# GELU of the w_in product: one ScalarE GELU from PSUM in place of four operations on two engines

## The chip, the core and the metric

The kernel runs on one core of one Trainium2 chip. The metric is the device time of one execution in microseconds (us). One core has several engines, each with its own instruction queue: TensorE (PE, matmuls), VectorE (DVE), ScalarE (ACT), GpSimd (POOL) and SyncE (SP, which starts most DMAs). VectorE and ScalarE take their queues in order. The Trainium skill says so ("TensorE: Matmul & The Clock Gate", section "Architectural detail: the array is 16× 32×32, not 1× 128×128": "ACT/DVE are strict FIFO").

## The reference

A transformer block on 2048 tokens of width 1024: an attention part (A), then a gated MLP (B). The change touches only the start of B, where `_gelu` is the tanh approximation:

```python
z  = gelu(layernorm(h) @ w_in, approximate=True)   # 2048 x 3584
z1 = z[..., :1792]
z2 = layernorm(z[..., 1792:])
g  = w_sp @ z2 + b_sp[:, None]                     # mixes tokens, w_sp is 2048 x 2048
out = h + (z1 * g) @ w_out
```

## The kernel before

The w_in stage works in four segments of 512 tokens. A segment has 30 blocks: 14 blocks "z1" (128 features x 512 tokens, written to their final place) and four token chunks of four blocks "z2" (128 tokens x 512, 512, 512 and 256 features). The four z2 blocks of a chunk go to one buffer, `Z2G`; then VectorE and GpSimd do the LayerNorm of the chunk (`z2_ln`), and the buffer is free again. Between two z2 chunks lie three or four z1 blocks. The units in `xu` make the next segment's input: `hn1` is its LayerNorm (VectorE), `hn2` its transposes (TensorE) and a copy (VectorE). There are 8 PSUM banks, taken in turn.

Each block is 8 matmuls into one bank. The GELU is then 0.5 x (1 + tanh(...)), with the factor 0.5 left for later:

```python
def z2_ln(tc, t4):                      # VectorE: 4 statistics, ..., normalise into Z2
    t = ln_stats(Z2G, 4, 4.0 * LN_EPS, [t4], csz=448)
    tz = P("dve", ... tensor_scalar(Z2[:, tc, :], Z2G[:], ...), waits=[t], sig=g_dve_pe)
    z2g_res.free = (g_dve_pe, tz[1])
# [cut]
blocks = z2blocks[0] + z1blocks[0:4] + z2blocks[1] + z1blocks[4:8] + z2blocks[2] + \
         z1blocks[8:11] + z2blocks[3] + z1blocks[11:14]
prev = None
for n in range(len(blocks) + 1):
    blk = blocks[n] if n < len(blocks) else None
    if prev is not None:                # second half of the GELU, block n-1
        # [cut]
        t3 = P("act", ... activation(TH[g], WG[g], Tanh, scale=GELU_C),
               waits=[prev["t2"], th_res[g].free], sig=g_act_dve)
        wg_res[g].free = t3
        t4 = P("dve", ... scalar_tensor_tensor(out, TH[g], 1.0, dst, add, mult),
               waits=[t3], sig=g_dve_pe)
        th_res[g].free = t4
        misc[prev["mb"]].free = t4      # the PSUM bank is free
        if prev["kind"] == "z2" and prev["fb"] == 3:
            z2_ln(prev["tc"], t4)
            if xu: xu.pop(0)()
    if blk is not None:                 # matmuls and first half, block n
        # [cut]
        w = [misc[mb].free] + (wready if n == 0 else [])
        if blk["kind"] == "z2" and blk["fb"] == 0:
            w.append(z2g_res.free)      # TensorE waits for the z2 buffer
        tp = proj8(blk["lhs"], blk["rhs"], dst, w, g_pe_act)
        # [cut]
        t1 = P("act", ... activation(X2T[g], dst, Square), waits=[tp, x2t_res[g].free], ...)
        t2 = P("dve", ... scalar_tensor_tensor(WG[g], X2T[g], GELU_K, dst, add, mult),
               waits=[t1, wg_res[g].free], ...)
        x2t_res[g].free = t2
        blk["t2"] = t2
    prev = blk
    if blk is not None and blk["kind"] == "z1" and blk["fc"] % 2 == 1 and xu:
        xu.pop(0)()
```

`P(engine, ...)` appends one instruction to the queue of that engine, with the semaphores it waits for. So the order in which the Python code calls `P` is the order of each queue.

The softmax here doesn't subtract the row's maximum and nothing guards it: scores larger than these inputs give would overflow.

## Time and profile before

| | before |
|---|---|
| median of the first 3 runs | 1267.02 us (1263.14 to 1269.56) |
| profiled run, span | 1264.5 us |
| attention and the first LayerNorm of B, 0 to 597.5 us | 597.5 us |
| w_in stage, 597.5 to 931.8 us | 334.3 us |
| loading and transposing of w_sp | 19.0 us |
| w_sp and w_out | 313.7 us |

First some lines of the profile page of before: busy time and share of the span by engine, the granted TensorE clock in 40 slices (in tenths), and the chain that ended last, by engine.

```profile
span 1264.5 us, 16478 instructions
...
PE 978.3 (77%) x6735; PEld 490.3 (39%) x6848; DVE 672.3 (53%) x1688; ACT 361.8 (29%) x502; POOL 35.1 (3%) x68
...
PEclk9979897998879986567978888889869999999999
...
PE 48%; DVE 31%; ACT 11%; issue 4%; DMA 4%; POOL 2%; SPq 0%; DVEq 0%; ACTq 0%; POOLq 0%
```

TensorE is at 77%, VectorE at 53% over the whole. The next view cuts the span into the four stretches of the table; the columns are length, busy time of each engine with the count of instructions, mean granted clock, DMA share and GB/s.

```profile
core 0: us, PE busy (x) PEld busy (x) DVE busy (x) ACT busy (x) POOL busy (x), PEclk, DMA share, GB/s
0.00:597.50 597.50, 434.24 (x4128) 234.82 (x4194) 316.24 (x1060) 234.72 (x262) 18.66 (x39) 0.84 0.15 51
597.50:931.80 334.30, 234.74 (x1035) 106.67 (x1054) 236.53 (x452) 127.09 (x240) 15.33 (x28) 0.85 0.03 8
931.80:950.80 19.00, 7.35 (x64) 6.72 (x66) 5.53 (x8) 0.00 (x0) 1.12 (x1) 0.50 0.94 340
950.80:1264.50 313.70, 301.97 (x1508) 142.05 (x1534) 113.95 (x168) 0.00 (x0) 0.00 (x0) 0.99 0.15 47
```

In the w_in stage TensorE and VectorE are equally busy, 70% and 71%, at a clock of 0.85. In the last stretch TensorE is busy 96% at 0.99.

One block, from the timeline (start, length, engine, and in brackets the idle time before and what ended it):

```profile
623.81 0.63 ACT L828 ACTIVATE th_116<-wg_114 128x512 bf16<-128x512 bf16 x1 [3.11 <-DVE wg_114 L862]
...
624.47 0.69 DVE L833 SCALAR_TENSOR_TENSOR z1T<-th_116,ps 128x512 bf16<-128x512 bf16 x1 [0.70 <-ACT th_116 L828]
625.08 0.68 DVE L862 SCALAR_TENSOR_TENSOR wg_115<-x2t_112,ps 128x512 bf16<-128x512 bf16 x1
625.68 0.68 DVE L765 COPY hnT_104<-ps 128x1024 bf16<-128x1024 bf16 x1
625.79 0.63 ACT L828 ACTIVATE th_117<-wg_115 128x512 bf16<-128x512 bf16 x1 [0.87 <-DVE wg_115 L862]
...
626.46 0.69 DVE L833 SCALAR_TENSOR_TENSOR z1T<-th_117,ps 128x512 bf16<-128x512 bf16 x1
```

`wg` is the first multiply-add (0.68 us), `th` the tanh on ScalarE (0.63), `z1T` the second multiply-add (0.69).

The chain of waits within the stage, by line (L328 is the LayerNorm statistics, L833 the second multiply-add, L862 the first, L828 the tanh), goes back and forth between VectorE and ScalarE:

```profile
by line: DVE stats L328 15.1%; DVE z2g L833 11.7%; DVE z1T L833 11.0%; ACT th_116 L828 11.0%; DVE wg_114 L862 10.4%; DVE wg_115 L862 10.1%; ACT th_117 L828 9.5%; POOL sm_58 L333 4.7%; DVE z_106 L791 3.6%; issue 3.5%; DVE mv L330 2.1%; PE ps
```

TensorE's largest waits in the same stage, and the place in the timeline that shows one of them:

```profile
PE ps L391 <- DVE z_106 L791: 65.7, 12, 6.4
PE ps L344 <- DVE hn_109 L751: 16.1, 3, 6.0
```

```profile
637.90 0.75 DVE L791 TENSOR_SCALAR z_106<-z2g,sm_58 128x1792 bf16<-128x1792 bf16 x1
...
638.79 1.44 PE L391 MATMUL ps<-w_in_hi,hnT_103 128*128 128x512 bf16 x3 [6.43 <-DVE z_106 L791]
```

The first matmul of a z2 chunk waits 6.43 us until the LayerNorm has read the buffer (`z_106`).

### The profile page before, as it was taken

The numbers are of one execution on the slowest core, as the hardware profiler recorded it, in microseconds if no ns is written. First come the engines' busy times: TensorE is split into PE (matmuls) and PEld (weight loads), VectorE is DVE, ScalarE is ACT, GpSimd is POOL, SyncE is SP. The second block draws the span as 40 slices with busy tenths as digits, with TensorE's granted clock in tenths as the row PEclk, the third lists the DMA queues.
The fourth block names the chain that finished last, engine by engine and source line by source line (L and its number), as shares of the span: only waits on it lengthen the run. The fifth ranks groups of instructions, "written<-read, shape, count | busy, mean of one in ns | idle before, by whom it ended". The sixth has DMA issues, their size and how long they took to land.

```text
span 1264.5 us, 16478 instructions
## 1 busy us (share of the span) xinstructions
PE 978.3 (77%) x6735; PEld 490.3 (39%) x6848; DVE 672.3 (53%) x1688; ACT 361.8 (29%) x502; POOL 35.1 (3%) x68
## 2 busy tenths in 40 slices
PE   3978785888669856674858676758639999999998
PEld 1444443443334423332423233323224445444443
DVE  4165426864577425654676777776644434244242
ACT  0357523663146405520334243334410000000000
POOL 2000000000000000000000000000000000000000
PEclk9979897998879986567978888889869999999999
DMA  8000012000300070002000000000042030120201
GB/s 315 1 26 1 1 34 68 1 1 1 101 1 2 2 282 18 1 18 91 18 17 1 17 18 9 9 1 1 1 179 83 5 109 26 50 88 5 68 1 59
DMA packets 23308, 54.56 MB, mean 43 GB/s; under 512 B 2368, under 2 KB 6976, under 8 KB 23232
## 3 DMA queue, kind: packets, MB, share of 16 engines
q1 hardware_dynamic: 19152, 34.10, 8.3%
q0 software_dynamic: 4080, 19.40, 4.1%
q8 instruction: 54, 0.88, 0.3%
q14 instruction: 22, 0.18, 0.0%
HBM read 45.10 MB, written 8.39 MB: 42 GB/s over the span
## 4 chain that ended last, share of the span: by engine, by line
PE 48%; DVE 31%; ACT 11%; issue 4%; DMA 4%; POOL 2%; SPq 0%; DVEq 0%; ACTq 0%; POOLq 0%
PE ps L391 16%; PE ps L945 15%; PE ps L972 8%; DVE stats L328 5%; ACT eall L525 4%; DVE z2g L833 3%; DVE z1T L833 3%; ACT th_116 L828 3%; DVE wg_114 L862 3%; DVE wg_115 L862 3%; ACT th_117 L828 3%; PE ps L518 2%; PE ps L511 2%; POOL sm_58 L333 2%; DMA wqkv<-in_A_wv_dram 2%
## 5 line engine op out<-in xcount | busy, mean ns | idle before, releaser
L525 ACT ACTIVATE eall<-ps 128x2048 bf16<-128x2048 f32 (+3 forms) x128 | 158.6, 1239 | 170.8 <-PE ps L518 170.1
L391 PE MATMUL ps<-xnT,wqkv 128*128 128x512 bf16 x489 | 118.8, 388 | 11.4 <-DVE msum L640 4.5
L972 PE MATMUL ps<-w_out,yT 128*128 128x512 bf16 x437 | 96.8, 379 | 6.9 <-DVE yT L951 6.4
L948 DVE TENSOR_TENSOR tmpg<-ps,brow_126 128x512 f32<-128x512 f32 x56 | 38.7, 691 | 117.5 <-PE ps L945 102.6
L945 PE MATMUL ps<-wspT_119,z_106 128*128 128x512 bf16 x439 | 98.2, 384 | 1.7 <-DVE wspT_119 L922 1.3
L945 PE MATMUL ps<-wspT_120,z_106 128*128 128x512 bf16 x440 | 96.6, 379 | 0.4
L391 PE MATMUL ps<-w_in_hi,hnT_104 128*128 128x512 bf16 (+1 forms) x253 | 63.1, 416 | 36.2 <-DVE z_106 L791 36.1
L391 PE MATMUL ps<-w_in_hi,hnT_103 128*128 128x512 bf16 (+1 forms) x251 | 63.4, 419 | 31.4 <-DVE z_106 L791 29.7
L391 PE MATMUL ps<-wo,oT 128*128 128x512 bf16 x248 | 63.4, 410 | 21.6 <-DVE oT L657 21.4
L828 ACT ACTIVATE th_116<-wg_114 128x512 bf16<-128x512 bf16 (+1 forms) x60 | 36.9, 615 | 134.9 <-DVE wg_114 L862 134.9
L391 PEld LDWEIGHTS ps<-xnT,wqkv 128*128 128x128 bf16 x512 | 47.4, 99 | 62.8 <-DVE msum L640 5.7
L972 PEld LDWEIGHTS ps<-w_out,yT 128*128 128x128 bf16 x448 | 43.5, 98 | 60.2 <-DVE yT L951 8.2
L945 PEld LDWEIGHTS ps<-wspT_119,z_106 128*128 128x128 bf16 x448 | 43.9, 99 | 53.2 <-issue 2.5
L945 PEld LDWEIGHTS ps<-wspT_120,z_106 128*128 128x128 bf16 x448 | 43.7, 98 | 51.9
L391 PE MATMUL ps<-wqkv,xnT 128*128 128x512 bf16 x248 | 58.7, 390 | 3.4 <-DVE msum L640 2.6
L518 PE MATMUL ps<-negtri,ident 128*128 128x128 bf16 x512 | 61.3, 255 | 0.0
L391 PEld LDWEIGHTS ps<-w_in_hi,hnT_104 128*128 128x128 bf16 x256 | 27.8, 111 | 73.2 <-DVE z_106 L791 39.6
L391 PE MATMUL ps<-hnT_103,w_in_lo 128*128 128x512 bf16 x218 | 52.4, 396 | 3.2 <-DVE z2g L833 3.0
L391 PEld LDWEIGHTS ps<-w_in_hi,hnT_103 128*128 128x128 bf16 x256 | 28.1, 112 | 68.3 <-DVE z_106 L791 32.7
L828 ACT ACTIVATE th_117<-wg_115 128x512 bf16<-128x512 bf16 (+1 forms) x60 | 35.2, 587 | 67.4 <-DVE wg_115 L862 67.4
L391 PE MATMUL ps<-hnT_104,w_in_lo 128*128 128x512 bf16 x217 | 51.1, 388 | 1.7 <-DVE z2g L833 1.3
L577 DVE TENSOR_SCALAR ps<-ps 128x4 f32<-128x4 f32 x96 | 16.1, 167 | 67.4 <-PE ps L556 64.4
(145 smaller groups left out, 1313.3 us busy)
## 6 DMA issues: line engine op xcount, KB each, us to landing
wspch_121<-in_B_w_sp_dram SPq DMA_DIRECT2D x8, 512.0 KB, 4.2
wspch_128<-in_B_w_sp_dram SPq DMA_DIRECT2D x8, 512.0 KB, 4.3
hr_0_127<-out_dram SPq DMA_DIRECT2D x16, 256.0 KB, 2.8
w_in_lo<-in_B_w_in_dram POOLq DMA_DIRECT2D x1, 3584.0 KB, 12.4
w_in_hi<-in_B_w_in_dram POOLq DMA_DIRECT2D x1, 3584.0 KB, 21.5
w_out<-in_B_w_out_dram POOLq DMA_DIRECT2D x1, 3584.0 KB, 17.9
xch_87<-in_A_x_dram SPq DMA_DIRECT2D x8, 256.0 KB, 2.8
xch_88<-in_A_x_dram SPq DMA_DIRECT2D x8, 256.0 KB, 3.0
```

What stands on the lines that cost most here:

```text
L328: t = P("dve", (lambda e, ci=ci: e.bn_stats(STATS[:, ci, :], eng_in_ap[:, ci * csz:(ci + 1) * csz])), waits=((list(first_wait) + [chain["l ...
L333: tp = P("pool", lambda e: e.tensor_tensor(SM4[:, 1:2], SM4[:, 0:1], MHALF[:], ALU.pow), waits=[t], sig=g_pool)
L391: tok = P("pe", (lambda e, i=i: e.matmul(dst, lhs_of_i(i), rhs_of_i(i), start=(i == 0), stop=(i == 7))), waits=(waits if i == 0 else []), ...
L511: P("pe", (lambda e, i=i, dst=dst: e.matmul(dst, kT[32 * i:32 * (i + 1), c, j * 128:(j + 1) * 128], qT[32 * i:32 * (i + 1), c, 128 * j:512 ...
L518: tp = P("pe", (lambda e, dstd=dstd: e.matmul(dstd, IDENT[:], NEGTRI[:], start=False, stop=True)), sig=(g_pe_act if i == 3 else None))
L525: ta = P("act", (lambda e: e.activation(dst4, src4, ACTF.Exp, scale=float(SCALE))), waits=wa, sig=g_act_pe)
L828: t3 = P("act", (lambda e, g=g, ncols=ncols: e.activation(TH[g][:, 0:ncols], WG[g][:, 0:ncols], ACTF.Tanh, scale=float(GELU_C))), waits=[p ...
L833: t4 = P("dve", (lambda e, g=g, ncols=ncols, dst=dst, o=prev["out"]: e.scalar_tensor_tensor(o, TH[g][:, 0:ncols], 1.0, dst, ALU.add, ALU.m ...
L862: t2 = P("dve", (lambda e, g=g, ncols=ncols, dst=dst: e.scalar_tensor_tensor(WG[g][:, 0:ncols], X2T[g][:, 0:ncols], float(GELU_K), dst, AL ...
L945: tok = P("pe", (lambda e, sc=sc, fc=fc, dst=dst: e.matmul(dst, Z2[:, sc, fc * 128:(fc + 1) * 128], wb[:, sc, :], start=(sc == 0), stop=(s ...
L948: t1 = P("dve", lambda e, dst=dst: e.tensor_tensor(TMPG[:], dst, BROW[0][:], ALU.add), waits=[tok, _w16(tb), tmpg_res.free], sig=g_dve_pe)
L972: tok = P("pe", (lambda e, fc=fc, half=half, tcl=tcl, dst=dst: e.matmul(dst, YT[:, fc, tcl * 128:(tcl + 1) * 128], WOUT[:, fc, half * 512: ...
```

## The change

The intent is to let ScalarE compute the GELU in one instruction that reads PSUM and writes bf16 to the final place, so that VectorE has no part in it. The scratch tiles go. The wait for the z2 buffer moves from TensorE's matmul to ScalarE's GELU, and the factor 0.5 at the end of the kernel becomes a plain addition. Cut to its core:

```diff
-        t = ln_stats(Z2G, 4, 4.0 * LN_EPS, [t4], csz=448)
+        t = ln_stats(Z2G, 4, LN_EPS, [t4], csz=448)
@@ the loop over the blocks
-                t3 = P("act", ... activation(TH[g], WG[g], ACTF.Tanh, scale=float(GELU_C)), ...)
-                t4 = P("dve", ... scalar_tensor_tensor(o, TH[g], 1.0, dst, ALU.add, ALU.mult), waits=[t3], ...)
-                [cut]
-                if blk["kind"] == "z2" and blk["fb"] == 0:
-                    w.append(z2g_res.free)
-                tp = proj8(blk["lhs"], blk["rhs"], dst, w, g_pe_act)
-                t1 = P("act", ... activation(X2T[g], dst, ACTF.Square), ...)
-                t2 = P("dve", ... scalar_tensor_tensor(WG[g], X2T[g], float(GELU_K), dst, ALU.add, ALU.mult), ...)
+            w = [misc[mb].free] + (wready if n == 0 else [])
+            tp = proj8(blk["lhs"], blk["rhs"], dst, w, g_pe_act)
+            wz = [z2g_res.free] if (blk["kind"] == "z2" and blk["fb"] == 0) else []
+            t4 = P("act", (lambda e, dst=dst, o=blk["out"]: e.activation(o, dst, ACTF.Gelu_apprx_tanh)),
+                   waits=[tp] + wz, sig=g_act_dve)
+            misc[mb].free = t4
@@ the last operation of the kernel
-                tf = P("dve", ... scalar_tensor_tensor(FIN2[half][:], dst, 0.5, HR2[b], ALU.mult, ALU.add))
+                tf = P("dve", ... tensor_tensor(FIN2[half][:], dst, HR2[b], ALU.add))
```

More of the change, by code (lines that the diff above doesn't have):

```diff
@@ L24 @@
 MEM_EPS = 1e-6
-GELU_C = 0.7978845608028654 * 0.044715
-GELU_K = 1.0 / 0.044715
 NJ = [512, 384, 256, 128]
@@ L244, in bass_sequential_preLN__memory_aug_infini_attn__mixer_gmlp__prompt_kernel @@
     HN = [tens("hn0", [128, D], BF16, R_CTMP + 4096), tens("hn1", [128, D], BF16, R_XN2)]
-    X2T = [tens("x2t%d" % i, [128, L], BF16, R_CTMP + 6144 + i * 1024) for i in range(2)]
     R_CT2 = R_HCH + 3072
     Z2G = tens("z2g", [128, FH], BF16, R_CT2)
-    WG = [tens("wg%d" % i, [128, L], BF16, R_CT2 + 3584 + i * 1024) for i in range(2)]
-    TH = [tens("th%d" % i, [128, L], BF16, R_CT2 + 5632 + i * 1024) for i in range(2)]
     WOUT = tens("w_out", [128, 14, D], BF16, R_WQKV)
@@ L773, in hn_chunk @@
         return hn2(tc)
-    x2t_res = [_Res(), _Res()]
-    wg_res = [_Res(), _Res()]
-    th_res = [_Res(), _Res()]
     z2g_res = _Res()
-    gctr = [0]
-    t_z1_done = {}
     hnt_ready = {}
@@ L820, in C1_seg @@
             z2blocks[3] + z1blocks[11:14]
-        prev = None
-        for n in range(len(blocks) + 1):
-            blk = blocks[n] if n < len(blocks) else None
-            if prev is not None:
-                g = prev["g"]
-                ncols = prev["ncols"]
-                dst = prev["dst"]
-                t3 = P("act", (lambda e, g=g, ncols=ncols: e.activation(TH[g][:, 0:ncols], WG[g][:, 0:ncols], ACTF.Tanh,
-                                                                    scale=float(GELU_C))),
-                       waits=[prev["t2"], th_res[g].free], sig=g_act_dve)
-                wg_res[g].free = t3
-                if prev["accum"] is None:
-                    t4 = P("dve", (lambda e, g=g, ncols=ncols, dst=dst, o=prev["out"]: e.scalar_tensor_tensor(
-                        o, TH[g][:, 0:ncols], 1.0, dst, ALU.add, ALU.mult)), waits=[t3], sig=g_dve_pe)
-                else:
-                    t4 = P("dve", (lambda e, g=g, ncols=ncols, dst=dst, o=prev["out"], ac=prev["accum"]:
-                                  e.scalar_tensor_tensor(o, TH[g][:, 0:ncols], 1.0, dst, ALU.add, ALU.mult,
-                                                         accum_out=ac)), waits=[t3], sig=g_dve_pe)
-                th_res[g].free = t4
-                misc[prev["mb"]].free = t4
-                if prev["kind"] == "z2" and prev["fb"] == 3:
-                    z2_ln(prev["tc"], t4)
-                    if xu:
-                        xu.pop(0)()
-            if blk is not None:
-                g = gctr[0] % 2
-                gctr[0] += 1
-                blk["g"] = g
-                mb = get_misc()
-                blk["mb"] = mb
-                ncols = blk["ncols"]
-                dst = bank_f32(mb)[:, 0:ncols]
-                blk["dst"] = dst
-                w = [misc[mb].free] + (wready if n == 0 else [])
-                if blk["kind"] == "z2" and blk["fb"] == 0:
-                    w.append(z2g_res.free)
-                tp = proj8(blk["lhs"], blk["rhs"], dst, w, g_pe_act)
-                if blk["kind"] == "z1" and blk["fc"] == 13:
-                    t_z1_done[s] = tp
-                t1 = P("act", (lambda e, g=g, ncols=ncols, dst=dst: e.activation(X2T[g][:, 0:ncols], dst, ACTF.Square)),
-                       waits=[tp, x2t_res[g].free], sig=g_act_dve)
-                t2 = P("dve", (lambda e, g=g, ncols=ncols, dst=dst: e.scalar_tensor_tensor(
-                    WG[g][:, 0:ncols], X2T[g][:, 0:ncols], float(GELU_K), dst, ALU.add, ALU.mult)),
-                       waits=[t1, wg_res[g].free], sig=g_dve_act)
-                x2t_res[g].free = t2
-                blk["t2"] = t2
-            prev = blk
-            if blk is not None and blk["kind"] == "z1" and blk["fc"] % 2 == 1 and xu:
@@ new lines, in C1_seg @@
+        for n, blk in enumerate(blocks):
+            mb = get_misc()
+            ncols = blk["ncols"]
+            dst = bank_f32(mb)[:, 0:ncols]
+            w = [misc[mb].free] + (wready if n == 0 else [])
[4 more added lines that the diff above has]
+            misc[mb].free = t4
+            if blk["kind"] == "z2" and blk["fb"] == 3:
+                z2_ln(blk["tc"], t4)
+                if xu:
+                    xu.pop(0)()
+            if blk["kind"] == "z1" and blk["fc"] % 2 == 1 and xu:
@@ L975, in C2C3_block @@
                             waits=(w if fc == 0 else []), sig=(g_pe_dve if fc == 13 else None))
-                tf = P("dve", (lambda e, half=half, dst=dst, b=b: e.scalar_tensor_tensor(
-                    FIN2[half][:], dst, 0.5, HR2[b][:, half * 512:(half + 1) * 512],
-                    ALU.mult, ALU.add)),
+                tf = P("dve", (lambda e, half=half, dst=dst, b=b: e.tensor_tensor(
+                    FIN2[half][:], dst, HR2[b][:, half * 512:(half + 1) * 512], ALU.add)),
                        waits=[tok, _w16(thr), fin_res[half].free], sig=g_dve_sp)
```

## The prediction

> **What bounds the kernel now.** In the timeline (span 1264.5 us) the w_in stage runs from the first w_in matmul at 597.5 us to the first w_sp load at 931.8 us: 334.2 us. In it the chain of waits hardly touches TensorE: it alternates between ScalarE (tanh, 20% of that window) and VectorE (the two multiply-adds, 43%; LayerNorm statistics, 15%). The table by stretches shows TensorE busy about 70% there, at a granted clock of 0.84 to 0.87; VectorE 70%. From 950 us TensorE bounds, at 0.97 to 1.00.
>
> Two things stall TensorE in the w_in stage (table of waits): the first z2 matmul of a token chunk waits for the previous z2 LayerNorm (65.7 us in 12 waits, up to 6.4 us), and transposes wait for the next segment's LayerNorm behind the same VectorE queue. After each stall, matmuls come every 0.427 us in place of 0.216 us for some microseconds.
>
> **What the change does.** For each of 30 blocks of a segment (26 of 512 columns, 4 of 256) it removes two VectorE operations (0.68 and 0.69 us; 0.41 and 0.42 at 256) and two ScalarE ones (Square 0.58, tanh 0.63), and adds one ScalarE GELU. The Trainium skill ("ScalarE: Activation LUTs", "ACT is a hardware spline evaluator") says that all functions cost the same per element; the trace agrees for Square and tanh (0.58 and 0.63 us), so I take 0.6 us. That page's "What ACT_TABLE_LOAD costs" puts a switch of sets at about 2.7 us; the compiled order has one new load, after the last exp, where ScalarE idles 49 us: hidden.
>
> Moved: the wait for the z2 buffer goes from TensorE's matmul to ScalarE's GELU, so TensorE may run ahead through the 8 PSUM banks. Dropping the final factor 0.5 saves nothing.
>
> **Cost of a segment afterwards.** TensorE: 208 matmuls of 512 columns at 0.216 = 44.9 us, 32 of 256 at 0.11 = 3.5, 32 transposes at 0.076 = 2.4; sum 50.8 us. VectorE: four z2 LayerNorms at 4.3 us, four input LayerNorms at 3.1, four copies at 0.7: 33 us. ScalarE: 26 x 0.6 + 4 x 0.4 = 17 us. TensorE becomes the bound. One stall stays: a segment's first transposes come 7 us after the z2 chunk ends, but VectorE needs 0.7 + 4.3 + 3.1 us: about 1.2 us, three times.
>
> Stage: 4 x 50.8 - 2.4 (last segment, no transposes) + 3.6 (stalls) + 2.5 (12 matmuls at half clock at the start) + 0.9 (last GELU) = 208 us, against 334. Nearly all removed work lay on the critical path, but the gain stops at TensorE's rate: 126 us. The other stages do not change.
>
> **Predicted: 1142 us, 80% between 1130 and 1160. Faster by over 2%: 0.98; within 2%: 0.015; slower: 0.005.**
>
> **What would show it.** Right: the w_in stage takes 205 to 215 us, granted clock there at least 0.96; the chain of waits runs through TensorE; waits of w_in matmuls for the z2 LayerNorm vanish; GELU takes 0.57 to 0.63 us; VectorE's busy time falls by about 155 us, ScalarE's by about 65 us. Wrong: GELU over 1 us; matmuls at 0.43 us inside segments; the stage over 225 us.
>
> **What would make it wrong.** The input LayerNorms queue behind z2 LayerNorms on VectorE worse than I count, stalling TensorE over 3 us per segment; dense matmuls with ScalarE and VectorE active get a lower clock; table loads between GELUs; bank waits.

## More of the kernel before

In VectorE's queue the two operations of one block stand next to each other, with the tanh on ScalarE between them.

What VectorE did in the 97.8 us in which it was not busy in the w_in stage is in its waits (kernel before, VectorE, w_in stage; columns: total us, times, longest):

```profile
engine line waited for: us in total, times, longest us
DVE z2g L833 <- ACT th_116 L828: 21.4, 32, 0.7
DVE z2g L833 <- ACT th_117 L828: 19.7, 32, 0.7
DVE z1T L833 <- ACT th_116 L828: 19.5, 28, 0.7
DVE sm_58 L335 <- POOL sm_58 L333: 18.5, 28, 0.7
DVE z1T L833 <- ACT th_117 L828: 9.0, 13, 0.7
DVE wg_114 L862 <- ACT x2t_111 L860: 4.3, 1, 4.3
```

It waited 69.6 us for the tanh (the four lines `th`), 18.5 us for GpSimd in the LayerNorms, and hardly ever for a Square, which is to say for TensorE. Busy time and these waits make up 330 us of 334: VectorE's queue was never short of work.

## The result, and the profile after

The changed kernel took 1140.81 us (median of 4 runs, 1138.74 to 1142.0), beside 1268.29 us for the kernel before (4 runs, 1263.14 to 1271.86). The ratio is 0.9003, with a 95% interval of 0.8973 to 0.9033.

The lines of the page of after that answer to those of before:

```profile
span 1140.2 us, 16027 instructions
...
PE 947.2 (83%) x6735; PEld 483.9 (42%) x6848; DVE 527.8 (46%) x1448; ACT 304.3 (27%) x383; POOL 35.2 (3%) x68
...
PEclk9988989798985999765678999999799999999999
...
PE 68%; DVE 15%; ACT 6%; DMA 4%; issue 4%; POOL 1%; SPq 0%; DVEq 0%; ACTq 0%; POOLq 0%
```

The four stretches of the changed kernel (same columns as before):

```profile
0.00:600.30 600.30, 436.27 (x4129) 235.58 (x4195) 316.62 (x1060) 236.08 (x263) 18.72 (x39) 0.84 0.15 51
600.30:806.30 206.00, 200.81 (x1035) 99.42 (x1054) 91.62 (x212) 68.24 (x120) 15.38 (x28) 0.99 0.05 14
806.30:825.50 19.20, 7.31 (x64) 6.68 (x66) 5.54 (x8) 0.00 (x0) 1.12 (x1) 0.69 0.95 339
825.50:1140.20 314.70, 302.82 (x1508) 142.19 (x1534) 114.03 (x168) 0.00 (x0) 0.00 (x0) 0.99 0.15 47
```

The w_in stage fell from 334.3 to 206.0 us, by 128.3 us. The other three stretches became 2.8, 0.2 and 1.0 us longer, so the span fell by 124.3 us. In the stage TensorE is now busy 97% at a clock of 0.99, and VectorE has 91.6 us of work where it had 236.5. What VectorE waits for has turned round (changed kernel, VectorE's waits in the w_in stage):

```profile
DVE stats L323 <- ACT z2g L818: 90.9, 16, 9.4
DVE sm_58 L330 <- POOL sm_58 L328: 18.5, 28, 0.7
```

It now waits 90.9 us for the next z2 chunk. TensorE's waits in the stage come to 4.6 us in all, 1.2 of them ahead of its first matmul:

```profile
PE ps L339 <- DVE hn_109 L746: 3.4, 3, 1.1
PE ps L386 <- DVE hnT_103 L760: 1.2, 1, 1.2
```

The timeline shows ScalarE's new work, the longest remaining wait of TensorE, and the matmuls after it:

```profile
610.55 0.60 ACT L818 ACTIVATE z1T<-ps 128x512 bf16<-128x512 f32 x1 [1.34 <-PE ps L386]
...
612.28 0.60 ACT L818 ACTIVATE z1T<-ps 128x512 bf16<-128x512 f32 x1 [1.13 <-PE ps L386]
...
616.82 0.62 PE L339 MATMUL ps<-ident,hn_109 128*128 128x128 bf16 x8 [1.13 <-DVE hn_109 L746]
...
617.28 6.22 PE L386 MATMUL ps<-w_in_hi,hnT_103 128*128 128x512 bf16 x32
```

A GELU takes 0.60 us, and TensorE delivers a block every 1.73 us (610.55 to 612.28). The wait of 1.13 us at 616.82 is for the next segment's normalised tokens; it comes three times. The 32 matmuls after it run at full rate: 6.22 us for 24 of 512 columns and 8 of 256.

The new table load of ScalarE is hidden (changed kernel, timeline of ScalarE):

```profile
553.92 0.60 ACT L520 ACTIVATE eall<-ps 128x512 bf16<-128x512 f32 x1 [0.92 <-PE ps L513]
554.54 1.28 ACT L818 ACT_TABLE_LOAD   x1
603.51 0.60 ACT L818 ACTIVATE z2g<-ps 128x512 bf16<-128x512 f32 x1 [47.70 <-PE ps L386]
```

It takes 1.28 us, directly after the last exp of the attention part, and 47.7 us of idle time follow. The chain of waits within the stage, by line (L386 is the matmul of the blocks), now runs along TensorE for 85% of it:

```profile
by line: PE ps L386 84.7%; DVE stats L323 5.1%; PE ps L339 2.9%; POOL sm_58 L328 1.6%; issue 1.4%; DVE z_106 L781 1.1%; DVE hn_109 L746 0.8%; DVE mv L325 0.7%; ACT z2g L818 0.6%; DVE sm_58 L330 0.5%; DVE sm_58 L326 0.5%; ACT z1T L818 0.3%;
```

### The profile page after: what moved, and what is told of

Read it like the earlier page. It is cut to its first block, busy times and chain, and to the rows that moved or that the text cites. A ratio compares the mean times of both kernels' runs of the same rounds, so it can differ in the third digit from the quotient of the medians. Undisturbed runs are those within 1.5% of the kernel's fastest.

```text
span 1140.2 us, 16027 instructions
## 1 busy us (share of the span) xinstructions
PE 947.2 (83%) x6735; PEld 483.9 (42%) x6848; DVE 527.8 (46%) x1448; ACT 304.3 (27%) x383; POOL 35.2 (3%) x68
## 4 chain that ended last, share of the span: by engine, by line
PE 68%; DVE 15%; ACT 6%; DMA 4%; issue 4%; POOL 1%; SPq 0%; DVEq 0%; ACTq 0%; POOLq 0%
PE ps L386 33%; PE ps L902 17%; PE ps L929 8%; ACT eall L520 4%; PE ps L513 3%; DVE stats L323 3%; PE ps L506 2%; DMA wqkv<-in_A_wv_dram 2%; PE ps L551 2%; PE ps L876 1%; DVE ta L579 1%; DVE tm L581 1%; POOL sm_58 L328 1%; PE ps L556 1%; PE ps L339 1%
## 5 line engine op out<-in xcount | busy, mean ns | idle before, releaser
L386 PE MATMUL ps<-xnT,wqkv 128*128 128x512 bf16 x489 | 118.6, 388 | 11.3 <-DVE msum L635 4.6
L386 PE MATMUL ps<-wo,oT 128*128 128x512 bf16 x248 | 63.9, 412 | 21.8 <-DVE oT L652 21.6
L323 DVE BATCH_NORM_STATS2 stats<-z2g 128x6 f32<-128x448 bf16 x64 | 35.3, 614 | 90.9 <-ACT z2g L818 90.9
L386 PEld LDWEIGHTS ps<-xnT,wqkv 128*128 128x128 bf16 x512 | 47.3, 99 | 62.4 <-DVE msum L635 5.8
L818 ACT ACTIVATE z2g<-ps 128x512 bf16<-128x512 f32 x64 | 34.8, 544 | 111.4 <-PE ps L386 111.4
L386 PE MATMUL ps<-wqkv,xnT 128*128 128x512 bf16 x248 | 59.0, 391 | 4.5 <-DVE msum L635 3.6
L506 PE MATMUL ps<-qT_70,kT_72 32*128 32x512 bf16 (+3 forms) x256 | 25.0, 380 | 33.6 <-ACT eall L520 33.6
L386 PE MATMUL ps<-w_in_hi,hnT_103 128*128 128x512 bf16 (+1 forms) x251 | 51.6, 364 | 1.4 <-DVE hnT_103 L760 1.2
L818 ACT ACTIVATE z1T<-ps 128x512 bf16<-128x512 f32 x56 | 33.4, 597 | 70.7 <-PE ps L386 70.7
L386 PE MATMUL ps<-hnT_104,w_in_lo 128*128 128x512 bf16 x217 | 49.4, 379 | 0.4
L386 PE MATMUL ps<-w_in_hi,hnT_104 128*128 128x512 bf16 (+1 forms) x253 | 49.6, 352 | 0.2
L386 PE MATMUL ps<-hnT_103,w_in_lo 128*128 128x512 bf16 x218 | 49.3, 379 | 0.3
L386 PEld LDWEIGHTS ps<-wo,oT 128*128 128x128 bf16 x256 | 25.6, 104 | 55.2 <-issue 13.4
```

The costliest lines, as they stand in the source:

```text
L323: t = P("dve", (lambda e, ci=ci: e.bn_stats(STATS[:, ci, :], eng_in_ap[:, ci * csz:(ci + 1) * csz])), waits=((list(first_wait) + [chain["l ...
L386: tok = P("pe", (lambda e, i=i: e.matmul(dst, lhs_of_i(i), rhs_of_i(i), start=(i == 0), stop=(i == 7))), waits=(waits if i == 0 else []), ...
L506: P("pe", (lambda e, i=i, dst=dst: e.matmul(dst, kT[32 * i:32 * (i + 1), c, j * 128:(j + 1) * 128], qT[32 * i:32 * (i + 1), c, 128 * j:512 ...
L818: t4 = P("act", (lambda e, dst=dst, o=blk["out"]: e.activation(o, dst, ACTF.Gelu_apprx_tanh)), waits=[tp] + wz, sig=g_act_dve)
```

## The experiments

Theory A: the w_in stage before was bound by VectorE's in-order queue, by its work together with the 0.7 us bubbles in which it waits for the tanh; with that work gone, TensorE's rate is the bound. Rival B: TensorE's own stalls at the z2 buffer, with the half-rate matmuls that follow them, bound the stage, and moving the wait to ScalarE was the gain. Rival C: the two ScalarE passes taken away were the gain.

Twelve kernels ran. All gave correct results but the ninth. Everything was timed against the kernel before, whose median was 1266.2 to 1266.9 us in each batch. "Stage" is the length of the w_in stage in the profiled run: 334.3 us before, 206.0 us after the change.

### 1. Kernel before, wait for the z2 buffer moved to VectorE

```diff
-                if blk["kind"] == "z2" and blk["fb"] == 0:
-                    w.append(z2g_res.free)
+                blk["zw"] = z2g_res.free if (z2, fb 0) else None
@@
-                    ... ALU.add, ALU.mult)), waits=[t3], sig=g_dve_pe)
+                    ... ALU.add, ALU.mult)), waits=[t3, prev["zw"]], sig=g_dve_pe)
```

> The kernel before, with only the wait for the free z2 buffer moved from TensorE's first matmul of a token chunk to VectorE's write of that buffer; the four-operation GELU stays. Theory A (VectorE's in-order queue, work plus the bubbles in which it waits for the tanh, bounds the w_in stage): the TensorE waits for the z2 LayerNorm (65.7 us) vanish or turn into waits for PSUM banks, the granted clock in the stage changes somewhat, but the time stays within 1% (1255 to 1275 us). Rival B (TensorE's stalls and the half-rate matmuls after them bound the stage): at least 60 us faster (below 1208 us).

Measured: 1268.05 us (ratio 1.0016, 0.9993 to 1.004). The stage, in one line of stretches (same columns):

```profile
597.30:932.00 334.70, 230.70 (x1056) 105.69 (x1056) 236.55 (x452) 127.23 (x240) 15.38 (x28) 0.86 0.03 9
```

The stage is 334.7 us, and VectorE's busy time is the same as before to 0.1 us. TensorE's waits for the LayerNorm are gone, and in their place it waits 46.6 us for PSUM banks that VectorE has not yet emptied. Moving the wait alone gives nothing.

### 2. Kernel before, TensorE kept busy ahead of the wait

```diff
+                if (z2, fb 0) and z2g_res.free is not None:
+                    fb_ = get_misc()
+                    for fi in range(20):
+                        P("pe", ... matmul(bank_f32(fb_), HNT[sbk][:, fi % 8, 0:128], HNT[sbk][:, fi % 8, :], start=True, stop=True))
```

> The kernel before, with 20 extra matmuls (result never read) ahead of each wait of TensorE for the z2 buffer, so that TensorE is not idle before the z2 blocks. Theory A: the matmuls at half rate inside segments become few and the granted clock in the stage rises from about 0.85 to over 0.93, but the time stays within 1% (1255 to 1278 us). Rival B: at least 20 us faster (below 1248 us), since the blocks after a stall take 1.7 us in place of 3.4.

Measured: 1271.1 us (ratio 1.0036, 1.0003 to 1.007).

```profile
603.80:938.40 334.60, 280.52 (x1356) 131.39 (x1356) 236.52 (x452) 127.21 (x240) 15.38 (x28) 0.93 0.03 9
```

The clock rose from 0.85 to 0.93 and TensorE did 46 us more of (useless) work, but the stage is 334.6 us. Half-rate matmuls cost nothing here either, because TensorE had time to spare. The few us more in the total are in the attention part, which took 603.8 us in this run in place of 597.5. With 1 and 2, rival B falls for the kernel before.

### 3. Kernel before, halves of the loop swapped

The block `if blk is not None:` (matmuls, Square, first multiply-add of block n) is put ahead of the block `if prev is not None:` (tanh, second multiply-add of block n-1). No instruction is added or taken away.

```diff
 for n in range(len(blocks) + 1):
-    if prev is not None: [second half, block n-1]
-    if blk is not None:  [matmuls and first half, block n]
+    if blk is not None:  [matmuls and first half, block n]
+    if prev is not None: [second half, block n-1]
```

> The kernel before, with the two halves of the block loop swapped: Square and the first multiply-add of block n are put in the queues before tanh and the last multiply-add of block n-1. The same instructions, but VectorE has the multiply-add of another block to do while ScalarE does the tanh. Theory A: VectorE's wait for the tanh (about 80 us in the stage) falls under 15 us and the stage takes VectorE's work alone, 62 us busy and about 6 us of waits for GpSimd per segment, so about 270 us in place of 334: 1195 to 1220 us. If work alone without bubbles were no bound (rival: only the latency of the four-step chain costs), the stage would fall to TensorE's 206 us: 1140 to 1150 us.

Measured: 1211.34 us (ratio 0.9579, 0.9552 to 0.9606), stage 277.8 us. All of VectorE's waits in the stage:

```profile
DVE wg L841 <- ACT x2t L839: 25.0, 34, 4.3
DVE sm L335 <- POOL sm L333: 18.5, 28, 0.7
```

The waits for the tanh have vanished from the list. In their place stand 25.0 us of waiting for a Square, which means for TensorE. The stage stayed far above the 206 us that the expectation gives for its rival, so the latency of the chain alone was not the bound: VectorE's work (229.7 us busy) and its waits make up 273 of 277.8 us.

### 4. Both: swapped, and the wait moved

> Both: halves swapped, and the wait for the z2 buffer moved to VectorE. Theory A: as with the halves swapped alone or up to 10 us faster, since VectorE's work stays the bound: 1190 to 1220 us. Rival B: clearly faster than the swap alone, by over 20 us.

Measured: 1188.7 us (ratio 0.9403, 0.9368 to 0.9437), stage 257.0 us. VectorE's waits:

```profile
DVE sm L335 <- POOL sm L333: 18.5, 28, 0.7
DVE wg L840 <- ACT x2t L838: 6.5, 5, 4.3
```

The wait for the z2 buffer, which cost nothing in the kernel before, is worth 20.8 us of the stage here. That is more than I expected from theory A (up to 10 us; the total is also 1.3 us under its range) and as much as I had put down for rival B: this expectation was a miss. The reason is in the two lists of waits: in experiment 3 VectorE runs dry while TensorE is held at the buffer (25.0 us), in experiment 4 it does not (6.5 us). Once the bubbles are gone, VectorE is fast enough for TensorE's hold-ups to reach it. So the same wait is free or costs 20 us, according to what else is slow. VectorE's work (227.2 us busy) and its waits now make up 252 of 257 us.

### 5. Changed kernel, wait for the z2 buffer back on TensorE

```diff
             w = [misc[mb].free] + (wready if n == 0 else [])
+            w += [z2g_res.free] if (z2, fb 0) else []
-            wz = [z2g_res.free] if (z2, fb 0) else []
@@
-                   waits=[tp] + wz, sig=g_act_dve)
+                   waits=[tp], sig=g_act_dve)
```

> The changed kernel, with the wait for the free z2 buffer put back on TensorE's first matmul of a token chunk. The z2 LayerNorm ends about 4.9 us after the last z2 matmul, and TensorE has 3 or 4 z1 blocks (5.2 or 6.9 us) to do in between. Theory A: at most 3 us slower than the changed kernel (1139 to 1146 us). Rival B (moving this wait is a large part of the gain): over 15 us slower (above 1156 us).

Measured: 1143.9 us (1138.5 to 1144.65; ratio to before 0.902, 0.8991 to 0.905), stage 206.1 us. In TensorE's waits the z2 buffer does not appear at all: the LayerNorm is done in time. In the changed kernel the place of this wait makes no difference (206.1 and 206.0 us).

### 6. Changed kernel, every GELU twice on ScalarE

```diff
+            t3 = P("act", ... activation(TH[0], dst, Gelu_apprx_tanh), waits=[tp, th_res[0].free], ...)
             t4 = P("act", ... activation(o, dst, Gelu_apprx_tanh), ...)
```

> The changed kernel, with every GELU done twice on ScalarE, the first into a scratch tile. ScalarE's busy time in the stage doubles, 68 to 136 us, as much as before the change. Theory A: nothing to speak of, 1139 to 1146 us (0.6 us more latency at a few hand-overs). Rival C (the ScalarE passes taken away are where the gain comes from): over 30 us slower.

Measured: 1140.99 us (ratio 0.9004, 0.8979 to 0.9029), stage 207.7 us. ScalarE's busy time in the stage rose from 68.2 to 121.7 us, nearly that of the kernel before (127.1), and nothing came of it but 1.1 us more of TensorE waiting for normalised tokens (4.5 in place of 3.4 us). Rival C falls as far as ScalarE's work goes. Its latency is another matter: it made the bubbles.

### 7 and 8. Changed kernel with one, and with two, VectorE passes per block

GELU writes a scratch tile. One VectorE operation (0 x PSUM + scratch, right in value and 0.69 us long like the old ones) moves it to its place; in 8 two such operations follow one another.

```diff
-            t4 = P("act", ... activation(o, dst, Gelu_apprx_tanh), waits=[tp] + wz, ...)
+            t3 = P("act", ... activation(TH[g], dst, Gelu_apprx_tanh), waits=[tp, th_res[g].free], ...)
+            t4 = P("dve", ... scalar_tensor_tensor(o, dst, 0.0, TH[g], mult, add), waits=[t3] + wz, ...)
+            th_res[g].free = t4
```

> The changed kernel, with GELU going to a scratch tile and one VectorE multiply-add per block (0 x PSUM + scratch, so the same values and the length of the old ones, 0.69 us) moving it to its place. VectorE's busy time per segment rises from 33 to about 52 us plus 6 us of GpSimd waits, against TensorE's 51 us. Theory A: about at the crossing of the two, 5 to 25 us slower than the changed kernel (1146 to 1166 us). Rival C: unchanged.

> As the run before with two such VectorE passes per block, as many as before the change, but no round trip between the engines. VectorE needs about 72 us per segment plus 6 us of GpSimd waits, less about 15 us in the last segment without input LayerNorms. Theory A: the stage takes 270 to 300 us, 1205 to 1235 us, near the run with the halves swapped. If it were the round trips between the engines and not VectorE's work, it would stay under 1170 us.

Measured: one pass 1142.95 us (ratio 0.9011, 0.8979 to 0.9043), two passes 1202.68 us (ratio 0.9491, 0.9465 to 0.9516). The stages, one pass first, then two:

```profile
600.90:809.80 208.90, 200.95 (x1035) 99.50 (x1054) 162.66 (x332) 67.91 (x120) 15.38 (x28) 0.99 0.05 13
```

```profile
598.30:868.40 270.10, 214.50 (x1035) 100.99 (x1054) 237.74 (x452) 68.25 (x120) 15.38 (x28) 0.92 0.03 10
```

The first pass added 71 us of VectorE work and 2.9 us to the stage; the second added 75 us of work and 61.2 us to the stage. With one pass VectorE's work and its 18.5 us of GpSimd waits come to 181 us, under TensorE's 201; with two they come to 256, over it. My expectation for 7 was a miss: I had put VectorE at 58 us a segment, because I counted the GpSimd waits twice and overlapping operations in full. In the measured numbers it is 45 us on average (181 / 4), and 48.5 in a segment that also makes the next one's input (43.2 busy and 5.3 of GpSimd waits, from 654.6 to 706.6 us; the last segment makes none). That is still under TensorE's 51, so the crossing lies a little above one pass. The two-pass run came in 2.3 us under the lower end of its range (1205), for the same reason, and is as theory A has it.

### 9. Changed kernel, seven of eight matmuls per block (wrong on purpose)

```diff
-            tp = proj8(blk["lhs"], blk["rhs"], dst, w, g_pe_act)
+            for i in range(7): tp = P("pe", ... matmul(dst, lh(i), rh(i), start=(i == 0), stop=(i == 6)))
```

> The changed kernel with seven in place of eight matmuls per w_in block; the result is wrong on purpose. GELU, LayerNorms and everything else stay. Theory A (after the change TensorE bounds the stage): 104 matmuls of 512 columns and 16 of 256 fall away at 0.216 and 0.11 us, 24 us; the stalls for the input LayerNorm grow by about 0.8 us per segment, since TensorE arrives earlier; so 20 to 24 us faster than the changed kernel, 1116 to 1122 us. If ScalarE or VectorE bounded it, the time would stay at 1141.

Measured: 1122.9 us (1117.9 to 1123.77; ratio 0.8853, 0.8825 to 0.8881), stage 188.0 us, 18.0 us less than the changed kernel; relative error 0.35, as intended. So TensorE is the bound after the change, though 18 is less than the 20 to 24 expected. TensorE's remaining wait, and some stretches of the stage with the granted clock (third column from the right):

```profile
PE ps L339 <- DVE hn L746: 6.0, 3, 2.0
```

```profile
615.00:622.00 7.00, 5.54 (x35) 3.02 (x36) 3.66 (x9) 1.65 (x4) 1.09 (x2) 1.00 0.26 76
...
662.00:669.00 7.00, 6.25 (x28) 2.77 (x29) 3.60 (x9) 1.19 (x2) 0.55 (x1) 0.76 0.26 75
...
709.00:716.00 7.00, 5.29 (x23) 2.36 (x24) 3.88 (x11) 0.96 (x2) 1.10 (x2) 0.76 0.20 56
```

The three waits grew from 1.13 to 1.99 us (6.0 in place of 3.4 us in all). After two of the three, in the stretches from 662 and from 709 us, the clock fell to 0.76 over 7 us, an estimated loss of 7 x 0.24 = 1.7 us each. So the 24.2 us of matmuls taken away (104 x 0.216 + 16 x 0.11), less 2.6 of longer waits and 3.4 of lost clock, give an estimate of 18.2 us, beside the measured 18.0. After waits of 1.13 us, in the changed kernel, the clock stayed at 1.00.

### 10, 11 and 12. Towards a faster kernel

What is left at TensorE's rate are the gaps: the three waits of 1.1 us in the stage, and the 19.2 us between the stage and the first w_sp matmul, in which TensorE waits for w_sp loads. Experiment 10 puts the first transposes of a segment one chunk later in TensorE's queue. Experiment 11 loads the first four w_sp chunks during the last w_in segment, into four places that are free by then; two of these (not one, as the expectation says) overlap scratch tiles that the change removed. Experiment 12 does both.

```diff
+            late, nxt = extra[2], extra[3]          # 10
+            extra[2] = lambda: None
+            extra[3] = lambda late=late, nxt=nxt: (late(), nxt())
@@
+        if s == NSEG - 1:                           # 11
+            for i, ch in enumerate(PRECH):
+                pre_tok.append(plan.dma("sp", ch[:], B_w_sp[i * 128:(i + 1) * 128, :], d_pre[i], waits=wpre))
         C1_seg(s, extra)
```

> The changed kernel with the first transposes of the next segment's tokens put after the second z2 chunk in TensorE's queue, one chunk later. The three waits of 1.1 us for the normalised tokens vanish; nothing else moves. Theory A: the w_in stage shortens by 3 to 3.5 us, to about 202.6 us; the whole about 1137 to 1138 us, inside the scatter of single runs, so the stage is to be read, not the total.

> The changed kernel with the first four w_sp chunks loaded during the last w_in segment, into four places that are free by then (one of them overlaps the scratch tiles that the change took away), in place of two at a time after the stage. The 19.2 us from the end of the w_in stage to the first w_sp matmul become the transposes and their eight VectorE copies, 8 x 0.85 us plus about 2 us: 8 to 10 us. So 9 to 11 us faster than the changed kernel, 1129 to 1133 us.

> Reordered transposes and early loads together: the two gains add, 12 to 14.5 us faster than the changed kernel, 1126 to 1130 us.

| | median us (range) | ratio to before (95%) | attention part | w_in stage | to first w_sp matmul |
|---|---|---|---|---|---|
| changed kernel | 1140.81 (1138.74 to 1142.0) | 0.9003 (0.8973 to 0.9033) | 600.3 | 206.0 | 19.2 |
| 10 reordered | 1132.48 (1131.58 to 1134.1) | 0.8938 (0.8916 to 0.896) | 595.0 | 201.7 | 18.7 |
| 11 early loads | 1124.43 (1122.56 to 1129.14) | 0.8884 (0.885 to 0.8917) | 596.9 | 206.4 | 5.7 |
| 12 both | 1118.92 (1117.14 to 1120.71) | 0.883 (0.8807 to 0.8853) | 596.8 | 201.8 | 5.7 |

The two gains add, as expected, and experiment 12 is the fastest kernel. The stage shortened by 4.3 us with the reordering (expected 3 to 3.5): the three waits, 3.4 us, are gone from TensorE's list, and the first 10 us ran at a clock of 0.80 in place of 0.75, an estimated 0.5 us; the rest was not traced. The gap shortened by 13.5 us with the early loads, more than the 9 to 11 expected: I had costed the eight VectorE copies at the 0.85 us that they take when they wait for TensorE, and back to back they took 4.87 us, 0.61 each.

All three totals came out under their expected ranges. They moved by more than these stretches, because the attention part, whose instructions are the same in all these kernels, took 3.4 to 5.3 us less in the profiled runs. Over the fourteen profiled runs it took from 595.0 to 603.8 us. In the traces the same small matmul groups there run at a higher rate now in one, now in the other: the same four matmuls of 256 columns took 0.40 us in the changed kernel and 0.29 in experiment 10 (at 76 us), and the next head group's four of 512 columns 0.40 and 0.61 (at 81 us). Why one build fares better than another with this was not tested, and stays open. A total that moves by less than about 9 us, the width of that spread, should be read by stages here.

## Why the prediction was right

- **The total.** Predicted 1142 us, measured 1140.81. The stage was put at 208 us against 334; measured 206.0 against 334.3. The gain was put at 126 us; 128.3 were found in the stage, of which 4.0 went to scatter in the other stretches.
- **The new bound.** TensorE's rate, 50.8 us a segment. Experiment 9 shows it directly (an eighth of the matmuls away, 18.0 us faster), and 6 and 7 show that neither ScalarE nor VectorE is near the bound any more: 53 us more of ScalarE work cost 1.7 us, and 71 us more of VectorE work cost 2.9 us.
- **The stall that stays.** Predicted about 1.2 us, three times; measured 1.13 us, three times. The start at half rate and the hidden table load are there as well, and the GELU of 512 columns takes 0.597 us on average (estimate 0.6). The terms hold one by one: at the first of these stalls the z2 LayerNorm took 4.30 us (estimate 4.3) and the input LayerNorm 3.13 (3.1).
- **The z2 wait.** Predicted to vanish from TensorE; it did. But experiment 5 shows that it vanishes wherever it is placed, because the LayerNorm is now in time.
- **VectorE's time was costed too high.** Busy time was to fall by about 155 us on VectorE and 65 us on ScalarE; the page shows 144.5 (672.3 to 527.8) and 57.5 (361.8 to 304.3). The counts were right; the sums of single durations are too large, because two operations that follow each other overlap in the trace (0.68 us long, started every 0.60), and busy time counts the overlap once. VectorE's 33 us a segment, GpSimd waits included, are measured as 31.1 in a segment that makes the next one's input (25.8 busy and 5.3 of waits, from 653.9 to 705.8 us), and as 27.5 on average ((91.6 + 18.5) / 4), since the last segment makes none. Neither mattered to the total, since TensorE was well above both.
- **One reason was too simple.** "Nearly all removed work lay on the critical path" holds, but work is not all of it. Experiments 3 and 4 keep every instruction of the old GELU and win 56.5 and 77.3 us of the stage by order alone. So of the 128.3 us, 77.3 are, taken in this order, to be had without taking any work away: that part is VectorE standing idle for the tanh (69.6 us of waits before, none after the swap), together with the z2 wait that starts to matter then. The other 51.0 us, from 257.0 to 206.0, need less VectorE work. The prediction also lists TensorE's stalls, though it notes that the chain hardly touches TensorE. The first of them cost nothing in the kernel before: experiment 1 removes the waits for the z2 LayerNorm, experiment 2 cuts them from 65.7 to 15.3 us and raises the clock, and neither gains anything. The other stall on the list, the transposes' wait for the input LayerNorm, was not removed by either; it grew from 16.1 to 27.3 and 19.0 us.

The Trainium skill's page "Perfetto Trace Analysis" (section "Identifying the Most-Contended Engine") says that the most-contended engine is the one with the highest occupancy, but that for TensorE the busy share of matmuls is a poor measure and the share of weight loads (with the rate of useful arithmetic, not worked out here) is to be used. By matmul busy time the stage before is a draw (70% for TensorE, 71% for VectorE); by weight loads (106.67 of 334.30 us, 32%) the page names VectorE, and the experiments agree. How an engine at 71% comes to be the bound is seen in its waits: 325 of 334 us were its work (236.5) or its waits for ScalarE's tanh and for GpSimd inside its own dependency chain (69.6 and 18.5).

## What to carry to other kernels

Ask of each stage which engine's queue is never short of work, counting its work and the waits for helpers inside its own chain; an engine at 71% can be the bound, and waits of another engine were then free, for as long as it stayed the bound (the z2 wait: nothing in experiment 1, 20.8 us once the bubbles were gone). Two dependent operations of one engine with a trip to another engine between them should not stand next to each other in an in-order queue: put another block's operation in between, which here won 57 us without changing an instruction. Fusing the chain paid down to the rate of the next engine and not further, so cost that engine first: here the first VectorE pass put back cost 2.9 us and the second 61.

## What the Trainium skill lacked or had wrong

- "TensorE: Matmul & The Clock Gate", section "HAM oscillation — how this bites in real kernels", gives as a rule no idle gaps of TensorE above about 3.4 us. Gaps of 1.99 us were followed by half rate in two of three cases (experiment 9, one profiled execution; clock 0.50 from 665 to 667 us, 0.76 over 7 us); gaps of 1.13 us in none of three (changed kernel).
- "ScalarE: Activation LUTs", section "What ACT_TABLE_LOAD costs", puts every switch to a different set at about 2.66 us, of which the load is 1.28. The load took 1.28 us here, as it says; the rest cannot be told, since ScalarE had nothing to do for 47.7 us after it. What the page lacks is that a switch can be free: the load was placed directly behind the last exp, and nothing waited for it.
- "Perfetto Trace Analysis", section "Identifying the Most-Contended Engine", says that for VectorE the occupancy is also a fair measure of how close one is to roofline. Nothing here speaks against it: 71% left room, and reordering alone took the stage from 334.3 to 277.8 us, beside VectorE's 236.5 us of work. What the section lacks is the sum that shows such an engine to set the pace: its work together with its waits for helpers inside its own chain, 325 of 334 us.
